# Four of six filter pieces laid out by a strided copy and a transposing DMA in place of TensorE transposes, with the first x loads moved ahead of the tables

## The chip, the cores and the metric

The kernel runs on one core of a Trainium2 chip. The metric is the device time of one execution in microseconds (us). Each number of a time below is the median of all executions, with the lowest and highest in brackets. Executions that lie over 1.5% above the fastest of the same kernel are called slow; they count in these medians, but they are left out of every ratio. The profile is one execution; its span is some 1.7 to 3.9 us shorter than the time of the same execution.

## The reference

Two independent halves share the core, and their outputs lie side by side.

```python
def _A_ref(q, k, v, shift_k, ssm_k, ssm_D):      # S = 2048, D = 576
    ... # k_shift: four taps of k along the sequence
    kv = k_shift * v
    L = 2 * S
    ... # kv and ssm_k padded to L, both through an FFT, multiplied, back
    y = y + kv * ssm_D[None, None, :]
    return q * y

def _B_ref(x, wqkv, wo):                          # 32 heads of 18
    ... # q, k, v = x @ wqkv
    phi = lambda t: jnp.where(t > 0, t + 1, jnp.exp(t)) + 1e-6
    pq, pk = phi(q), phi(k)
    kv = jnp.einsum("bhsd,bhse->bhde", pk, v)
    ... # num, den, o = num / den
    return o... @ wo
```

The first half is a long convolution. The kernel computes it with matmuls against tables of cosines and sines. For these the filter `ssm_k`, which lies in memory as channels by time, must be brought into a form with time on the partitions. The second half is linear attention: projections of x, an exponential, and small matmuls.

## The kernel before

The program first makes a list of some 550 operations. Two tables that were tuned together with it then say in which order and on which engine each is issued (`PLAN`) and where each buffer lies (`PLACES`). Each engine works through its own operations in the order of the plan.

The filter comes in six pieces of 96 channels and 2048 time steps (`hs`). A piece needs time step 16a+b to go to partition a and slot b. Before, TensorE does this with 16 transposes, each of which reads 128 elements 16 apart, in two groups of eight. ScalarE or VectorE then evicts each group from PSUM into `hT`:

```python
def h_piece(i):
    cc, hh = i // 2, i % 2
    hs = SB("hs", [96, S])
    load("hs", hs, lambda e: dma(hs.t[:], A_ssm_k[96 * i:96 * i + 96, :], e), 393216, ..., two=i < 2)
    for half in range(2):
        ps = psb(1, "hps")
        def tr(e, half=half, ps=ps):
            ...
            hv = hs.t[:].rearrange("d (a b) -> d b a", b=16)
            for j in range(8):
                nc.tensor.transpose(out=o[:, 128 * j:128 * j + 96], in_=hv[:, 8 * half + j, :], ...)
        def ev(e, half=half, ps=ps):
            ...
            copy(e, hT[cc].t[:, 8 * half:8 * half + 8, 96 * hh:96 * hh + 96], i_)
    ...  # one small add (hD) of the term D into time step 0
```

The copy helper chooses the engine's instruction:

```python
def copy(e, o, i):
    if e == "ACT":
        nc.scalar.activation(out=o, in_=i, func=ACTF.Copy)
    else:
        nc.vector.tensor_copy(out=o, in_=i)
```

In the front, the loads of x wait for a memset of one column of the same buffer (`after=[x1]`), and TensorE multiplies by a dummy operand between its first operations so that its clock stays up. `SPIN` says how many such fillers, in units of 128 columns, stand at each place:

```python
x1 = P.op(("POOL", 0.2), lambda e: nc.gpsimd.memset(x_sb.t[:, :, D:D + 1], 1.0), ..., name="x1")
SPIN = (32, 2, 2, 2, 2, 2, 2, 2, 2, 2, 2, 2, 2, 2)
```

From some 16 us on, TensorE's projections of k and q (`wk`, `wq`) interleave with the convolution. Each group of a k projection needs ScalarE to take an exponential of it out of PSUM (`ek`) and then VectorE to finish it (`pk`). Both also read PSUM, so TensorE's next group waits until VectorE is done.

## Time and profile before

| | before |
|---|---|
| time, us | 171.67 (171.38 to 171.68) |
| span of the profile, us | 171.2 |
| TensorE busy | 160.8 us, 94% |
| VectorE busy | 141.6 us, 83% |
| ScalarE busy | 112.8 us, 66% |
| bytes moved | 37.7 MB |

The view is of busy time in windows. Its columns are the window, its length, then busy time and count of instructions for TensorE, its weight loads, VectorE, ScalarE and GpSimd, then the granted clock, the DMA share and GB/s.

```profile
47.00:60.00 13.00, 12.73 (x120) 9.38 (x119) 12.58 (x15) 10.37 (x14) 5.57 (x2) 1.00 0.90 254
72.00:86.00 14.00, 14.00 (x140) 11.20 (x138) 12.68 (x11) 5.58 (x7) 0.00 (x0) 0.97 0.81 211
```

Between 47 and 60 us ScalarE has 13.00 - 10.37 = 2.6 us free. Some 2.1 us of its work there are evictions of the filter (`hT`), which the change removes. Between 72 and 86 us it has 8.4 us free.

### The profile page before, as it was taken

Reading aid. Unit: us, or ns where it says so; the run is one execution under the profiler, and the core shown is the slowest. Engines: PE = TensorE matmul, PEld = TensorE weight load, DVE = VectorE, ACT = ScalarE, POOL = GpSimd, SP = SyncE. Lnnn points to the kernel's source line nnn. Section 1 sums busy time; section 2 is a strip of 40 time slices with the busy share of each in tenths; the row PEclk is TensorE's granted clock in tenths of the full one; section 3 lists DMA queues with packets and bytes.
Section 4 is the critical chain, followed back from the end, with each engine's and each line's share of the span. In section 5 each row is a group of like instructions: output and inputs, shape, how many; then the busy total and the mean of one; then the engine's idle time right before and its main releaser. Section 6 shows DMA issues by size and latency. Waiting matters only on the chain.

```text
span 171.2 us, 3899 instructions
## 1 busy us (share of the span) xinstructions
PE 160.8 (94%) x1622; PEld 119.5 (70%) x1622; DVE 141.6 (83%) x141; ACT 112.8 (66%) x122; POOL 40.8 (24%) x28
## 2 busy tenths in 40 slices
PE   7799999999999997899999997998999999999991
PEld 2479876677667865688867885785656489978670
DVE  0224689999899999999799979899989999596690
ACT  0525965483768879735376399999999997745301
POOL 8600000800070520000069027000268000810000
PEclk9957999999999999699999999999999999999999
DMA  5999997999999623399200179999988488995375
GB/s 133 281 319 325 415 357 106 208 312 316 244 242 349 180 56 122 69 297 258 84 4 7 54 217 262 246 169 268 251 271 339 165 311 272 339 304 157 110 228 162
DMA packets 53423, 37.71 MB, mean 220 GB/s; under 512 B 32991, under 2 KB 49501, under 8 KB 52894
## 3 DMA queue, kind: packets, MB, share of 16 engines
q1 hardware_dynamic: 52574, 36.50, 76.8%
q10 hardware_dynamic: 832, 0.97, 2.3%
q8 instruction: 12, 0.20, 0.5%
q14 instruction: 5, 0.04, 0.1%
HBM read 20.16 MB, written 4.98 MB: 147 GB/s over the span
## 4 chain that ended last, share of the span: by engine, by line
PE 66%; ACT 9%; DVE 8%; DMA 6%; SPq 5%; issue 4%; ACTq 0%; DVEq 0%
PE ps_all L678 13%; PE ps_all L854 11%; PE ps_all L657 9%; PE ps_all L606 8%; PE ps_all L631 6%; PE ps_all L513 5%; PE ps_all L711 5%; DVE m L261 4%; DMA hs<-in_A_ssm_k_dram 4%; ACT Ch L254 3%; PE ps_all L564 3%; SPq L528 3%; DMA X<-sph 2%; SPq L246 2%; ACT Cu L254 2%
## 5 line engine op out<-in xcount | busy, mean ns | idle before, releaser
L261 POOL TENSOR_TENSOR v<-m,v 128x1536 bf16<-128x1536 bf16 x4 | 12.4, 3098 | 69.5 <-DVE m L261 69.5
L261 POOL TENSOR_TENSOR sph<-spu,sph 128x2048 bf16<-128x2048 bf16 x4 | 16.3, 4070 | 32.1 <-DVE pqT L841 16.8
L711 PE MATMUL ps_all<-pk,x_sb 128*128 128x288 bf16 (+1 forms) x160 | 22.0, 298 | 0.0
L854 PE MATMUL ps_all<-M,pqT 126*128 126x288 bf16 (+1 forms) x160 | 21.7, 286 | 0.0
L261 DVE TENSOR_TENSOR m<-kh,Wj 128x3072 bf16<-128x3072 bf16 x12 | 20.8, 1750 | 0.1
L513 PEld LDWEIGHTS <-Gsb 128*128 128x128 bf16 x240 | 16.7, 100 | 6.0 <-issue 3.7
L678 PE MATMUL ps_all<-xT,wq 128*126 128x512 bf16 (+1 forms) x80 | 20.5, 379 | 0.1
L657 PE MATMUL ps_all<-wk,xT 128*128 128x288 bf16 x128 | 20.1, 286 | 0.0
L711 PEld LDWEIGHTS <-x_sb 128*128 128x128 bf16 x160 | 16.2, 102 | 4.9 <-issue 0.2
L854 PEld LDWEIGHTS <-pqT 126*128 126x128 bf16 (+1 forms) x160 | 14.8, 97 | 5.7 <-issue 2.1
L678 PEld LDWEIGHTS <-wq 128*126 128x126 bf16 (+1 forms) x100 | 13.0, 131 | 7.8 <-issue 0.4
L254 ACT ACTIVATE Vt<-ps_all 128x1024 bf16<-128x1024 f32 x15 | 14.9, 1029 | 4.9 <-PE ps_all L606 3.2
L682 ACT ACTIVATE eq<-ps_all,neg 126x1024 bf16<-126x1024 f32 (+1 forms) x10 | 11.1, 1113 | 10.5 <-PE ps_all L678 10.5
L254 ACT ACTIVATE Ch<-ps_all 128x1536 bf16<-128x1536 f32 x11 | 16.2, 1511 | 2.4 <-PE ps_all L513 2.3
L606 PE MATMUL ps_all<-cst,sph 128*128 128x128 bf16 x144 | 17.1, 219 | 0.1
L606 PE MATMUL ps_all<-cst,X 128*128 128x128 bf16 x144 | 17.0, 219 | 0.0
L261 DVE TENSOR_TENSOR m<-m 128x3072 bf16<-128x3072 bf16 (+1 forms) x12 | 16.2, 1346 | 0.1
L254 ACT ACTIVATE Cu<-ps_all 128x1536 bf16<-128x1536 f32 x10 | 15.1, 1535 | 1.4 <-PE ps_all L513 1.3
L254 ACT ACTIVATE ob<-ps_all 128x576 bf16<-128x576 f32 x13 | 8.6, 663 | 9.9 <-PE ps_all L854 9.8
L657 PEld LDWEIGHTS <-xT 128*128 128x128 bf16 x128 | 12.2, 98 | 4.1 <-issue 0.8
L254 ACT ACTIVATE spu<-ps_all 128x1024 bf16<-128x1024 f32 x13 | 13.1, 1033 | 2.2 <-PE ps_all L557 2.2
L606 PEld LDWEIGHTS <-X 128*128 128x128 bf16 x144 | 14.1, 98 | 0.7 <-issue 0.3
(87 smaller groups left out, 294.5 us busy)
## 6 DMA issues: line engine op xcount, KB each, us to landing
X<-sph SPq DMA_DIRECT2D x18, 256.0 KB
hs<-in_A_ssm_k_dram SPq DMA_DIRECT2D x6, 384.0 KB
v<-in_A_v_dram SPq DMA_DIRECT2D x2, 1152.0 KB
out_dram<-ob SPq DMA_DIRECT2D x16, 144.0 KB
bct<-rden_rows SPq DMA_DIRECT2D x8, 252.0 KB
kh<-in_A_k_dram SPq DMA_DIRECT2D x1, 1584.0 KB
q<-in_A_q_dram SPq DMA_DIRECT2D x1, 1280.0 KB
out_dram<-q SPq DMA_DIRECT2D x4, 320.0 KB
```

The lines of the kernel that those rows point to most:

```text
L254: nc.scalar.activation(out=o, in_=i, func=ACTF.Copy)
L261: last[e] = (nc.gpsimd if e == "POOL" else nc.vector).tensor_tensor(**kw)
L513: nc.tensor.matmul(ps.t[:, bank, lo - 512 * bank:hi - 512 * bank], lhsT=Gsb.t[:, ri, bg, j, :], rhs=src[:, lo - CC * j:hi - CC * j], start ...
L528: load(name, None, lambda e: nc.sync.dma_start_transpose(out=dst(), in_=src()), 524288, rd=rd, wr=wr, bias=bias, issue=1.8, row=512, gap=0.3)
L564: nc.tensor.matmul(ps.t[64 * h:64 * h + 64, r, :].rearrange("p (b k) -> p b k", b=4), lhsT=W2D()[64 * r:64 * r + 64, :], rhs=cv[64 * r:64 ...
L606: nc.tensor.matmul(ps.t[:, j // 4, 128 * (j % 4):128 * (j % 4) + 128], lhsT=src.t[:, 8 * jp + j, :], rhs=W3(wi), start=(wi == 0), stop=(wi ...
L631: nc.tensor.matmul(o, lhsT=Esb.t[:, b, ri, :], rhs=vt[:, 2 * b + ri], start=(ri == 0), stop=(ri == 1))
L657: nc.tensor.matmul(ps.t[:, hh, 0:HALF], lhsT=xs(t, 128 * r, 128), rhs=wk.t[:, t, HALF * hh:HALF * hh + HALF], start=(t == 0), stop=(t == 4))
L678: nc.tensor.matmul(ps.t[0:hn, j, :], lhsT=wq.t[:, t, h0:h0 + hn], rhs=xs(t, 1024 * gp + 512 * j, 512), start=(t == 0), stop=(t == 4))
L682: P.op(("ACT", _act(1024) + 0.09), lambda e: nc.scalar.activation(out=eb.t[0:hn], in_=ps.t[0:hn], func=ACTF.Exp, bias=neg1.t[0:hn, :]), rd ...
L711: nc.tensor.matmul(ps.t[:, hh, 0:n], lhsT=x_sb.t[:, r, FT[t]:FT[t] + 128], rhs=pk.t[:, r, HALF * hh:HALF * hh + n], start=(r == 0), stop=( ...
L854: nc.tensor.matmul(ps.t[:, hh, 0:HALF], lhsT=pqT.t[0:hn, c, 128 * r:128 * r + 128], rhs=M.t[0:hn, c, HALF * hh:HALF * hh + HALF], start=(c ...
```

## The change

The intent is to take four of the six pieces off TensorE, which is the fullest engine. ScalarE permutes each piece in SBUF with one copy, and a transposing DMA (a "turn") then brings it into `hT`. Besides, the first x rows are loaded before the tables, the memset that held them comes first, only the smallest loads are issued by ScalarE, some memsets go to VectorE, one output block is cut in two, and the fillers are set anew. The whole order is tuned again.

```diff
-        return P.op({"SP": issue, "ACT": 0.52} if two else ("SP", issue), fn, ...
+        return P.op(("ACT", 0.52) if two and nb < 80000 else ("SP", issue), fn, ...
...
-        for half in range(2):
+        if i >= HP:
+            hp = SB("hp", [96, 16, 128])
+            P.op({"ACT": 0.1 + 2048 * 0.00084, "DVE": _dve(2048)}, lambda e: copy(e, hp.t[:], hs.t[:].rearrange("d (a b) -> d b a", b=16)),
+                 rd=[hs], wr=[hp], name="hperm", bias=("t%d" % cc, 0.0))
+            load("hturn", None, lambda e: nc.sync.dma_start_transpose(
+                out=hT[cc].t[:, :, 96 * hh:96 * hh + 96], in_=hp.t[:].rearrange("d b a -> d (b a)")), 393216, rd=[hp], ...
+        for half in range(2) if i < HP else ():
...
-SPIN = (32, 2, 2, 2, 2, 2, 2, 2, 2, 2, 2, 2, 2, 2)
+SPIN = (28, 1, 7, 1, 1, 1, 15, 1, 1, 1, 1, 9, 10, 1, 1, 3)
-PORT = ("tapv", "p1", "p2", "hD")
+PORT = ("tap+", "tapv", "p1", "p2", "hD")
+HP = 2
... (memsets with a choice of engine; the last output block in halves; PLAN and PLACES replaced whole)
```

## The prediction

> **What bounds the kernel now.** I read the page of the profile first (busy shares, slices), then the chain that ended last in order of time, then busy time in windows cut where that chain changes engine, then groups of instructions, and last the load queue in order of time.
>
> The slices, 4.28 us each:
>
> ```profile
> PE   7799999999999997899999997998999999999991
> DVE  0224689999899999999799979899989999596690
> ACT  0525965483768879735376399999999997745301
> PEclk9957999999999999699999999999999999999999
> DMA  5999997999999623399200179999988488995375
> ```
>
> TensorE is the first bound: nine tenths or more almost throughout. VectorE is nearly full from slice 6 to slice 33, ScalarE only from slice 23 to 33, and the load queue is full up to slice 13. The clock is low in slices 2, 3 and 16.
>
> The chain that ended last, from its start and from the middle:
>
> ```profile
> 2.19 6.00 DMA hs<-in_A_ssm_k_dram
> ...
> 11.61 1.28 PE ps_all L513 x10
> ...
> 15.55 0.67 PE ps_all L513 x10
> 16.33 1.23 PE ps_all L657 x10
> ...
> 97.99 0.48 PE ps_all L483 x8
> ...
> 100.75 0.14 ACT hT L254
> ```
>
> The reader is to see three things. The front waits for the first filter pieces (hs). The same ten matmuls of L513 take 1.28 us at 11.61 and 0.67 at 15.55: the front runs at half clock. Filter transposes (L483) and their evictions (hT) stand on the chain. The first k projection (L657) begins at 16.2 and the last matmul ends at 167.7, which leaves 3.5 us for the last eviction and store.
>
> Windows (columns: length; busy us and count for PE, PEld, DVE, ACT, POOL; granted clock; DMA share; GB/s):
>
> ```profile
> 66.15:70.00 3.85, 2.03 (x25) 1.64 (x22) 3.85 (x3) 3.85 (x4) 0.00 (x0) 0.93 0.02 6
> 99.15:117.26 18.11, 15.78 (x226) 12.94 (x225) 16.26 (x17) 17.93 (x17) 4.40 (x2) 1.00 0.96 233
> ```
>
> TensorE stands idle for 1.8 us in the first of these, waiting for ScalarE's evictions of 1.5 us each, and for 2.3 us in the second, where ScalarE is full.
>
> To turn this into a budget I summed TensorE's work from the first k projection on, each kind at its warm step in the chain: 16 k at 1.23, 10 q at 2.16, 5 G at 4.05, 16 out at 1.24, 18 i1 at 0.89, i2 9.0 in all, 22 s1 at 0.67, 36 s2 at about 0.35, 8 filter-transpose groups at 0.55, 4 x-transpose groups 1.1, kv, z, den and M 4.0. The sum is 143.1 us. Between 16.2 and 167.7 lie 151.5, so 8.4 us are bubbles and slow clock. Of these the windows show 4.8 as idle TensorE, and about 1.4 is the low clock after 70 us (32 matmuls of G took 5.50 us there and 4.11 later). So: 16.2 + 143.1 + 8.4 + 3.5 = 171.2, the span.
>
> **What the Trainium skill says.** "TensorE: Matmul & The Clock Gate", Part 1: the array runs at half clock by default and is released only after a window of some 3.4 us of sustained work. The trace agrees: the granted clock is 0.50 from 8.5 to 12.8 us, after TensorE had been idle for half of 6.4 to 8.5, and 1.00 from 15. "DMA: Bandwidth & Descriptors", section "Issuing engines are not separate DMA queues": issuing from several engines saves sequencer time only. The trace fits: the issues on ScalarE's queue took 0.2 to 0.6 us each, so moving a few of them is worth little by itself. "Advanced Engine Details and Errata", section "X-Bar Transpose (TRN2)", says transposing DMAs are as fast as plain ones. Here the trace differs: while the two transposing loads of x held the queue (26 to 30 us) only 105 GB/s moved, against 437 from 19 to 22. The measurement decides: a turn costs more of the queue than its bytes suggest.
>
> **The change, part by part.**
>
> Filter pieces. Each of six pieces is now 16 transposes and two evictions. Their groups:
>
> ```profile
> L483 PE MATMUL ps_all<-cst,hs 96*128 96x96 bf16 x96 | 8.0, 235 | 1.1 <-DMA hs<-in_A_ssm_k_dram 1.1
> L254 ACT ACTIVATE hT<-ps_all 128x768 bf16<-128x768 bf16 x6 | 4.6, 808 | 0.2 <-PE ps_all L483 0.2
> L256 DVE COPY hT<-ps_all 128x768 bf16<-128x768 bf16 x6 | 3.3, 552 | 7.3 <-PE ps_all L483 7.3
> ```
>
> Four pieces leave this path: 8 groups of 8 transposes, each 0.48 to 0.63 us on the chain, so 8 x 0.55 = 4.4 us of TensorE. All eight lie after 55 us, where nothing but TensorE's partners bounds it, so I count all 4.4. Evictions removed, by the new program order: ScalarE 4 x 0.81 = 3.2 us, VectorE 4 x 0.55 = 2.2. Added: four permuting copies of 96x2048, all on ScalarE. Its copies cost 0.81 us for 768 elements and 1.02 for 1024, so some 0.83 ns each, which makes 1.9 us a copy and 7.5 in all. They are issued among the k and q projections before 62 us, where ScalarE is busy 22.3 of 34.6 us (16.3 to 50.9): mostly hidden. Also added: four turns of 0.39 MB; turns of 0.52 MB took about 2.1 us to issue when the queue was not full. Say 2 us each, 8 us of queue. Two are needed by about 57 us, near the end of the load-bound stretch; the other two fall where the DMA share was 0.02 to 0.44.
>
> The front. The load queue before:
>
> ```profile
> 2.19 0.60 SPq L246 DMA_DIRECT2D hs<-in_A_ssm_k_dram  x1
> ...
> 4.21 0.16 POOL L308 MEMSET x_sb<- 128x16 bf16 x1
> ...
> 4.39 0.64 SPq L246 DMA_DIRECT2D x_sb<-in_B_x_dram  x1
> ```
>
> The queue stood for 1.6 us because the x loads waited for a GpSimd memset; the change makes that memset GpSimd's first operation. The new order is tables for the transpose, hs twice, all four first x loads, two pieces of G, part of k, wk. Up to wk that is 3.8 MB. At the pace of before (0.57 MB by 4.28, 1.75 by 8.5, 3.13 by 12.8, 3.88 by 15) this has landed at 14.8; the filled gap gives back some 0.5 us. TensorE can then be through with both x groups, and k begins at about 14.6 instead of 16.2: 1.6 us. The remaining work also loses the second x group, 1.1 us, which is done ahead of k in otherwise waiting time. The fillers (matmuls that keep the clock) go from 58 to 82 units of 128 columns, now put before the operations that wait for x; if they keep the clock high, the half-clock phase disappears, and the k start is limited by data alone.
>
> The middle. The first convolution input lands ahead of wk, and two taps now precede the first k evacuation on VectorE, which before sat idle a good part of the time up to 19.1 us, when its first tap ran. VectorE was then full to 86 us, and its chain led to the wait at 50 to 60 us. A start some 5 us earlier plus 2.2 us less work moves its convolutions ahead. Three small adds move to GpSimd (3.1 us each there, 0.95 on VectorE) in exchange for three products coming back: no net change. The eviction of one filter spectrum in that stretch goes to VectorE, which should take away the stall at 66 to 70 (1.9 us) and the low clock after it (1.4 us). The denominator chain comes after two G products instead of three, so the multiplication of the second output starts earlier than its 117 us.
>
> The end. The last block of the second inverse is cut in two, with smaller last stores, but the last instruction is again an output store of the attention half: the 3.5 us of tail stay.
>
> Sum: k start 14.6; work 143.1 - 4.4 - 1.1 = 137.6; bubbles 8.4 - 3.3 + 3.0 = 8.1, where 3.0 is my allowance for new waits on permuting copies, turns and a fuller ScalarE; tail 3.5. The span is 163.8, and with the 0.5 us by which the median of before exceeded its span, 164.3 us.
>
> **Rivals.** First, the turns become the bound: the copy must wait for its hs, which lands behind 11 MB of loads; ScalarE runs in order, so an early copy stalls all k and q evacuations, and the turns of the second filter block hold up the loads queued behind them. For: the queue is full to 57 us and transposes are slow. Against: the two hs loads now stand ahead of the three turns that filled the queue from 36.9 to 49. This would cost 3 to 5 us and give 167 to 169. Second, the front gains nothing: TensorE falls to half clock because x is late, as it did at 8.5 us; the front's work and fillers then stretch by about 3 us, to 167. Third, ScalarE sets the pace from 100 to 145 us whatever TensorE has to do (43.1 of 45 us busy); then the 4.4 us come back as bubbles and only the front's gain and the relief of two evictions remain: 168. Fourth, the other way: VectorE's earlier start empties nearly all bubbles, and the time is 160 to 161.
>
> **Range and chances.** The sum has most of its weight on removed work that I can count, so faster by over 2% (below 168.2) needs only 3.5 of some 7.4 us. One rival alone keeps it near the border; two together reach "same". I say 160.5 to 168.8, faster 0.79, same 0.18, slower 0.03.
>
> **What would show it.** Right: L483 with 32 matmuls instead of 96; first L657 matmul at 14 to 15 us; clock of the third and fourth slices at 8 or more; no idle gap of TensorE near the third filter spectrum; ScalarE's permuting copies at 1.9 us with little wait before them; last matmul at about 160. Wrong: copies waiting for hs, a wait of L513 for a turn, a first k after 16 us, or ScalarE full for 45 us again with more TensorE idle than 2.3 us beside it.

## More of the kernel before

A letter in the plan is the engine: P for TensorE, A for ScalarE, D for VectorE, G for GpSimd, S for the load queue.

The profile of before fell in an execution of 174.28 us, called slow.

## The result, and the profile after

| | before | after |
|---|---|---|
| time, us | 171.68 (171.38 to 172.14) | 177.38 (176.76 to 179.94) |
| span of the profile, us | 171.2 | 175.0 |
| TensorE busy, us | 160.8 | 158.6 |
| ScalarE busy, us | 112.8 | 125.6 |
| bytes moved, MB | 37.7 | 39.3 |

The changed kernel is slower: the ratio is 1.032, with an interval of 1.027 to 1.037. Ratios here are the mean time of one kernel's fast runs over the mean of the other's fast runs in the same rounds, so they are not quite the ratio of the medians. The prediction said 164.3 and a range up to 168.8. The median lies 13.1 us above the prediction and 8.6 us above its range. The profile of after is of the run of 176.76, a fast one.

The slices of the profile after, each 4.4 us long, in tenths:

```profile
PE   7999999999989397979699997889999999999991
DVE  7138995998994799895599799899998999785791
ACT  2639847556699868999886766999899869735201
PEclk9969999999999789999999999999999999999999
DMA  5999999999944598197983379999999889935355
```

Two dents are new. In slice 14 (57 to 61 us) TensorE is at 3 tenths, and the clock is at 7 and 8 tenths in slices 14 and 15. In slices 18 to 20 (74 to 87 us) TensorE, which was full there before, shows 7, 9 and 6, and VectorE falls to 5 in two of them. ScalarE is at 8 or 9 tenths beside both dents.

The groups of instructions that answer to those shown of before (columns: line, engine, operation, what is written and read, count, then busy us, mean ns, and the idle time before them):

```profile
L254 ACT ACTIVATE hp<-hs 96x2048 bf16<-96x2048 bf16 x4 | 15.8, 3956 | 0.0
...
L493 PE MATMUL ps_all<-cst,hs 96*128 96x96 bf16 x32 | 2.7, 253 | 0.0
...
L254 ACT ACTIVATE hT<-ps_all 128x768 bf16<-128x768 bf16 x2 | 1.5, 808 | 0.4 <-PE ps_all L493 0.4
```

TensorE's filter transposes went from 96 to 32, as meant. ScalarE lost four evictions of 0.81 us. It gained four copies of 3.96 us each, 15.8 us in all, where the prediction had 7.5. There is no idle time before them, so they did not wait for their data.

The windows that answer to those of before:

```profile
47.00:60.00 13.00, 9.62 (x71) 6.55 (x69) 9.45 (x10) 12.70 (x10) 3.67 (x2) 0.97 0.54 92
72.00:86.00 14.00, 10.85 (x121) 8.15 (x124) 9.74 (x10) 13.60 (x10) 0.37 (x1) 1.00 0.80 151
```

ScalarE is now the full engine in both. TensorE lost 12.73 - 9.62 = 3.1 us of work in the first and 14.00 - 10.85 = 3.2 us in the second; VectorE lost about as much in each.

How one copy does it is seen in the timeline of the first dent (start, duration, instruction, and in brackets the idle time before it with what ended it):

```profile
47.16 3.97 ACT L254 ACTIVATE hp<-hs 96x2048 bf16<-96x2048 bf16 x1
...
53.28 3.91 ACT L254 ACTIVATE hp<-hs 96x2048 bf16<-96x2048 bf16 x1
...
57.85 1.42 DVE L681 SCALAR_TENSOR_TENSOR pk<-ek,ps_all 128x576 bf16<-128x576 bf16 x2 [3.18 <-ACT ek L678]
...
59.32 1.07 PE L574 MATMUL ps_all<-ctH,cst 64*64 64x512 bf16 x8 [2.65 <-DVE pk L681]
```

The second copy holds ScalarE from 53.28 to 57.19. Four exponentials of k projections (`ek`) queue up behind it. VectorE sits idle for 3.18 us until the first of them is done, and TensorE for 2.65 us until VectorE has emptied its PSUM. The clock then follows: from 60 to 65 us it was 0.74.

The chain that ended last, in the second dent (start, duration, what):

```profile
72.40 3.98 ACT hp L254
76.38 1.40 ACT Cu L254
77.77 0.90 ACT sph L254
78.67 3.84 ACT hp L254
82.52 1.34 ACT Cu L254
```

Here the copies themselves stand on the path, end to end with evictions that TensorE waits for: 11.5 us of the chain on ScalarE alone.

To see where the lead was won and lost, I counted TensorE's remaining useful work at several moments. Every matmul that is still to come counts with its duration at full clock, and fillers count nothing. The total is 146.7 us before and 142.3 us after, so by this count the removed transposes are worth 4.4 us, as predicted. The column "before" is its second profile. (A count made again from the traces, with somewhat other durations, gives leads that differ by up to 0.3 us.)

| at, us | before | after | copies in order (e2) | copies shared (e12) |
|---|---|---|---|---|
| 25 | 131.7 | 127.5 | 127.3 | 126.2 |
| 47 | 109.5 | 105.8 | 105.5 | 104.6 |
| 60 | 97.0 | 96.7 | 93.7 | 94.7 |
| 72 | 88.7 | 88.1 | 84.0 | 85.1 |
| 86 | 74.9 | 78.1 | 70.3 | 73.1 |
| 145 | 20.0 | 24.1 | 15.8 | 18.6 |

At 47 us the changed kernel is 3.7 us ahead. Between 47 and 60 us it loses 3.4, and between 72 and 86 us it loses 3.8. It ends some 4 us behind. Those two stretches hold the four copies. The profiles are not typical runs: those of e2 and e12 are of the fastest execution of each, and that of before is of one at 172.82 us. So the lead of e2 at the end of the table, some 4 us, is more than the 2.9 us between the medians.

Last, the front. The load queue after (start, duration, issue):

```profile
2.11 1.28 SPq L246 DMA_DIRECT2D x_sb<-in_B_x_dram  x2
...
9.37 0.39 SPq L246 DMA_DIRECT2D wk<-in_B_wqkv_dram  x1
```

The first x loads are issued at 2.11 us instead of 4.39. But the load of wk, which the first k projection needs, is issued at 9.37 us instead of 5.96. The first k matmul started at 16.31 us, against 16.17 before. The prediction had 14.6.

### The profile page after: what moved, and what is told of

Read it like the earlier page. It is cut to its first block, busy times and chain, and to the rows that moved or that the text cites. A ratio compares the mean times of both kernels' runs of the same rounds, so it can differ in the third digit from the quotient of the medians.

```text
span 175.0 us, 3767 instructions
## 1 busy us (share of the span) xinstructions
PE 158.6 (91%) x1561; PEld 113.7 (65%) x1561; DVE 143.4 (82%) x142; ACT 125.6 (72%) x123; POOL 36.7 (21%) x23
## 4 chain that ended last, share of the span: by engine, by line
PE 46%; ACT 14%; DVE 3%; issue 2%; ACTq 0%; DVEq 0%
PE ps_all L870 11%; PE ps_all L616 9%; PE ps_all L727 7%; PE ps_all L646 6%; PE ps_all L523 5%; ACT hp L254 4%; PE ps_all L574 3%; ACT Cu L254 3%; ACT Ch L254 3%; PE ps_all L673 2%; ACT sph L254 2%; DVE pk L681 2%; PE ps_all L694 1%; PE ps_all L567 1%; ACT ob L254 1%
## 5 line engine op out<-in xcount | busy, mean ns | idle before, releaser
L870 PE MATMUL ps_all<-M,pqT 126*128 126x288 bf16 (+1 forms) x160 | 21.5, 286 | 0.1
L727 PE MATMUL ps_all<-pk,x_sb 128*128 128x288 bf16 (+1 forms) x160 | 20.5, 286 | 0.3 <-ACT Ch L254 0.2
L254 ACT ACTIVATE Vt<-ps_all 128x1024 bf16<-128x1024 f32 x14 | 13.8, 1025 | 6.6 <-DVE q L651 3.0
L673 PEld LDWEIGHTS <-xT 128*128 128x128 bf16 x128 | 12.8, 100 | 7.4 <-issue 3.2
L254 ACT ACTIVATE Cu<-ps_all 128x1536 bf16<-128x1536 f32 x11 | 16.1, 1500 | 0.7 <-PE ps_all L523 0.4
L264 POOL TENSOR_TENSOR X<-spu,X 128x2048 bf16<-128x2048 bf16 x3 | 12.2, 4075 | 20.7 <-DVE pqT L857 16.9
L254 ACT ACTIVATE hp<-hs 96x2048 bf16<-96x2048 bf16 x4 | 15.8, 3956 | 0.0
L254 ACT ACTIVATE Ch<-ps_all 128x1536 bf16<-128x1536 f32 x10 | 14.9, 1502 | 1.0 <-PE ps_all L523 1.0
L254 ACT ACTIVATE ob<-ps_all 128x576 bf16<-128x576 f32 x12 | 7.6, 652 | 10.3 <-PE ps_all L870 9.4
L681 DVE SCALAR_TENSOR_TENSOR pk<-ek,ps_all 128x576 bf16<-128x576 bf16 x16 | 11.9, 750 | 3.7 <-ACT ek L678 3.6
L678 ACT ACTIVATE ek<-ps_all,neg 128x576 bf16<-128x576 f32 x16 | 11.5, 737 | 4.8 <-PE ps_all L673 4.6
L254 ACT ACTIVATE sph<-ps_all 128x1024 bf16<-128x1024 f32 x14 | 14.0, 1023 | 1.1 <-PE ps_all L574 0.7
```

What stands on the lines that cost most here:

```text
L264: last[e] = (nc.gpsimd if e == "POOL" else nc.vector).tensor_tensor(**kw)
L673: nc.tensor.matmul(ps.t[:, hh, 0:HALF], lhsT=xs(t, 128 * r, 128), rhs=wk.t[:, t, HALF * hh:HALF * hh + HALF], start=(t == 0), stop=(t == 4))
L678: P.op(("ACT", _act(576) + 0.085), lambda e: nc.scalar.activation(out=eb.t[:], in_=ps.t[:, :, 0:HALF], func=ACTF.Exp, bias=neg1.t[:]), rd= ...
L681: P.op(("DVE", _dve(576)), lambda e: nc.vector.scalar_tensor_tensor(out=pk.t[:, r, 0:D].rearrange("p (h c) -> p h c", h=2), in0=eb.t[:], s ...
L727: nc.tensor.matmul(ps.t[:, hh, 0:n], lhsT=x_sb.t[:, r, FT[t]:FT[t] + 128], rhs=pk.t[:, r, HALF * hh:HALF * hh + n], start=(r == 0), stop=( ...
L870: nc.tensor.matmul(ps.t[:, hh, 0:HALF], lhsT=pqT.t[0:hn, c, 128 * r:128 * r + 128], rhs=M.t[0:hn, c, HALF * hh:HALF * hh + HALF], start=(c ...
```

## The experiments

The first theory, called A, is that the copies' own length on ScalarE costs the time. The rivals are that the turns and the fuller load queue cost it, that the front with its fillers does, and that the new order of the program does whatever the copies take (C). For e5 to e7 three of the seven executions of before were slow.

**e1_before.** No edit: the kernel before again, for a second profile.

> The kernel before, unchanged, for a profile in its fast state (the one at hand is from a run of 174.28 us, over its median of 171.67). Both theories: span about 170 us, no low clock near 70 us, first k projection at 16.2 us, last matmul near 166.5.

Measured: 172.82 us, one run, span 170.8, clock 0.97. The low clock in slice 17 (68 to 73 us; the prediction counts from 0 and calls it 16) is there again, at 6 tenths, so this expectation was wrong: it belongs to the kernel, not to a disturbed run. In its windows TensorE was busy 12.74 us of 47 to 60 and 13.82 us of 72 to 86, nearly as in the first profile, so the two dents of after are not an accident of the profile compared with.

**e2_flat.** The four copies read in order. The result is wrong, because the filter's time steps then go to wrong places. The automatic comparison with the reference passed it all the same; the likely reason is that this half of the output is small beside the tolerance. It is no valid version and serves for its time alone. It also means that the comparison cannot tell whether a version is right; for those called valid below this rests on reading the code.

```diff
-  copy(e, hp.t[:], hs.t[:].rearrange("d (a b) -> d b a", b=16))
+  copy(e, hp.t[:], hs.t[:].rearrange("d (b a) -> d b a", b=16))
```

> The changed kernel with the permuting copy reading its 2048 elements in order instead of 16 apart (result wrong on purpose; same engine, same place, same turns). Theory A (the strided reads make each copy 3.97 us, and ScalarE's in-order queue holds back the projections' evictions): copies take 1.9 us, the idle TensorE at 55-60 and 80-85 us shrinks by more than half, time 171 to 173.5. Rival B (TensorE waits for the turns or their loads, not for the copies): time within 1 us of the changed kernel, 176.4 to 178.4. Rival C (the new order itself is worse): also above 175.

Measured: 169.14 us (168.50 to 169.95), ratio 0.981 (0.975 to 0.987). The tile's own view gives the lowest, median and highest duration in ns, and the windows show what follows:

```profile
L254 ACT ACTIVATE hp<-hs x4: 1895/1897/1898, 46.9 to 71.8; 96x2048 bf16<-96x2048 bf16 x4
```

```profile
47.00:60.00 13.00, 12.19 (x90) 8.13 (x89) 13.00 (x13) 11.97 (x14) 3.98 (x3) 1.00 0.93 186
72.00:86.00 14.00, 14.00 (x176) 11.14 (x174) 13.84 (x14) 10.95 (x11) 1.03 (x2) 1.00 0.98 196
```

The same instruction on the same bytes took 1.90 us instead of 3.97 when it read in order. TensorE is back at 12.19 us in the first window and full in the second, the mean clock is 1.00, and the lead of 4 us lasts to the end (table above). Order of the program, turns, loads and fillers are those of after. So rival C and the turns cannot explain the loss: 177.38 - 169.14 = 8.2 us hang on the copies' length. The two medians are of different rounds; the ratios to before, 1.032 and 0.981, differ by 5.1% of 172, or 8.7 us, which agrees. The time is below the 171 to 173.5 that theory A expected: the length cost more than A had reckoned.

**e3_dve.** The four copies issued by VectorE at the same places of the plan.

```diff
- A320 ... A316 ... A347 ... A351
+ D320 ... D316 ... D347 ... D351
```

> The changed kernel with the four permuting copies on VectorE at the same places of the order. Theory A: a copy takes some 2.2 us there[...], ScalarE is freed of 15.8 us, VectorE gets 9 us more; time 170 to 173.5. Rival B: unchanged, 176.4 to 178.4. Rival C: above 175.

Measured: 178.43 us (178.21 to 178.56), ratio 1.035 (1.028 to 1.042).

```profile
L256 DVE COPY hp<-hs x4: 1996/2030/2753, 48.7 to 78.5; 96x2048 bf16<-96x2048 bf16 x4
```

```profile
56.10 1.12 PE L673 MATMUL ps_all<-wk,xT 128*128 128x288 bf16 x4 [2.86 <-DVE pk L681]
```

VectorE does the strided copy in 2.03 us, half of ScalarE's time, and yet the kernel is as slow as after. VectorE was full in this stretch without them (12.58 of 13 us before), and the second copy (53.39 to 55.39 us) again stands in front of the `pk` that frees TensorE's PSUM. A's expectation was missed: it is not the duration alone that counts but what else the engine has to do in that window.

**e4_pe.** The four pieces go back to TensorE, in the order of after, with one eviction for each piece.

```diff
-  hp = SB("hp", [96, 16, 128])
-  ... hperm on ScalarE, hturn on the load queue
+  hp = psb(2, "hps")
+  ... 16 transposes into hp, then one eviction of 1536 elements (two on VectorE, two on ScalarE)
```

> The changed kernel's order and front with the four pieces turned on TensorE again (16 transposes and one eviction of 1536 elements each, two on VectorE, two on ScalarE) at about the places of the copies; no copies, no turns. Theory A: TensorE gets 4.4 us more work and loses the stalls of some 8 us: 171 to 174. Rival C (the rest of the new order is worse than the old): above 175. If the rest of the new order is worth something by itself, below 170.

Measured: 181.25 us (180.87 to 181.99), ratio 1.052 (1.045 to 1.058). In TensorE's timeline:

```profile
51.46 0.65 PE L681 MATMUL ps_all<-wk,xT 128*128 128x288 bf16 x4 [1.05 <-DVE hT L256]
...
57.60 0.65 PE L681 MATMUL ps_all<-wk,xT 128*128 128x288 bf16 x4 [1.54 <-ACT hT L254]
```

TensorE waits for the evictions that I placed by hand behind VectorE's taps, in PSUM that the next projection needs. This run says that those places are bad, not that the rest of the new order is. I count it as a failed test of C. e2_flat is the test that holds.

**e5_write_strided.** The copy reads in order and writes 128 elements apart. By its access patterns it moves each element to the same place as in after.

```diff
-  copy(e, hp.t[:], hs.t[:].rearrange("d (a b) -> d b a", b=16))
+  copy(e, hp.t[:].rearrange("d b a -> d a b"), hs.t[:].rearrange("d (a b) -> d a b", b=16))
```

> The changed kernel with the permuting copy turned about: it reads hs in order and writes 128 elements apart, instead of reading 16 apart and writing in order; same result, still on ScalarE. If only strided reads are slow on ScalarE, a copy takes 1.9 us and the time is that of the copy without a stride, 168 to 170. Rival (any stride is slow there): 3.5 to 4 us a copy and 176 to 178.

Measured: 201.31 us (200.25 to 201.85), ratio 1.178 (1.168 to 1.187).

```profile
L254 ACT ACTIVATE hp<-hs x4: 9302/9327/9346, 47.1 to 95.6; 96x2048 bf16<-96x2048 bf16 x4
```

Both expectations were missed. This strided writing costs 9.33 us a copy, 4.6 ns an element, against 1.9 ns for the strided reading and 0.93 ns in order. The strides differ too (128 elements against 16), so whether the writing or the wider step costs more is not separated. The four copies grew by 4 x 5.4 = 21.5 us and the kernel by 201.31 - 177.38 = 23.9 us. With e2_flat this gives three points: 1.90, 3.97 and 9.33 us a copy make 169.1, 177.4 and 201.3 us. From the first to the second the time rises by 8.2 us for 8.3 us of copies. Nearly every microsecond of copy beyond 1.9 comes out at the end.

**e6_pool.** The copies on GpSimd, which is the emptiest engine.

```diff
+  elif e == "POOL":
+      nc.gpsimd.tensor_copy(out=o, in_=i)
- A320 ... A316 ... A347 ... A351
+ G320 ... G316 ... G347 ... G351
```

> The changed kernel with the four copies on GpSimd at the same places. Theory A (what costs is the time in which an engine that evicts the projections is held): GpSimd evicts nothing, so even a copy of 4 to 5 us is hidden, except that one small add and one hT correction queue behind it; 167.5 to 171. If the turns' lateness counts instead, L523 waits for hT and the time is above 173.

Measured: 183.31 us (182.14 to 184.21), ratio 1.071 (1.060 to 1.082). VectorE's groups in the window from 40 to 52 us, while the first two copies ran:

```profile
L266 DVE TENSOR_TENSOR v<-m,v 128x1536 bf16<-128x1536 bf16 x1 | 4.0, 4017 | 0.0
```

A's expectation of 167.5 to 171 us was missed by far. The copies took 3.90 to 5.43 us each on GpSimd, and meanwhile VectorE's product of two SBUF operands took 4.02 us instead of 0.95. One tap took 5.45 us instead of 1.75. "SBUF — State Buffer" of the Trainium skill, section "Who interferes with whom", says that a VectorE instruction with two SBUF inputs contends with a GpSimd instruction that reads SBUF. The trace agrees, with these numbers: the product began at 41.67 us, under the first copy. The rival of that expectation, that lateness of the turns counts, finds no support: in the trace's list of waits no product of the filter (L525) waits for a turn. That the held-up VectorE is what makes the whole kernel slow is read from the trace and not shown by a run of its own. The first copy started at 40.95 us, after waiting 1.47 us for `hs`: the data are there six microseconds before ScalarE's first copy of 47.16, so a late `hs` is not what delays after. After itself shows no idle time before its copies either.

**e7_split.** The first two copies in quarters of 512 elements, with ScalarE's evictions between them.

```diff
- A320 ... A316
+ A320.0 ... A320.1 ... A320.2 ... A320.3 ... (A316 likewise, evictions between)
```

> The changed kernel with the first two copies cut into quarters, each quarter followed by one of the next evictions of ScalarE; the same elements at the same stride, so the same total of some 4 us a piece plus about 0.15 us of start-up for each quarter; the two later copies are whole. If head-of-line blocking is what hurts (an eviction stuck behind 3.97 us), the gap at 55 to 60 us mostly goes: 173.5 to 175.5. If the total of ScalarE's time is what hurts, no gain: 176.5 to 178.5.

Measured: 177.31 us (176.69 to 178.25), ratio 1.037 (1.028 to 1.045).

```profile
47.00:60.00 13.00, 9.95 (x74) 6.96 (x73) 10.85 (x12) 13.00 (x16) 3.41 (x2) 0.97 0.44 71
```

Nothing is gained. ScalarE is now busy all 13.00 us, and TensorE is where it was (9.95). The first dent is therefore not only a long instruction that blocks the ones behind it. ScalarE simply has more to do there than fits: before it was busy 10.37 us, some 2.1 us of `hT` evictions go, and two whole copies add 7.9, eight quarters of some 1.15 us even 9.2.

**e8_front.** The copies as in after, and the fillers cut.

```diff
-SPIN = (28, 1, 7, 1, 1, 1, 15, 1, 1, 1, 1, 9, 10, 1, 1, 3)
+SPIN = (28, 1, 1, 1, 1, 1, 1, 1, 1, 1, 1, 1, 1, 1, 1, 1)
```

> The changed kernel with the fillers of the front cut to one unit each after the first 28 (12 units of 512 columns and 7 of 128 fewer). If the x pieces had landed and the fillers themselves held TensorE back, the first transpose of x comes before 10 us and k starts at 15 or before. If the loads set it, the first x transpose stays at about 11 us, k at about 16.3, with more idle TensorE or half clock before it.

Measured: 176.33 us, one run. TensorE's timeline:

```profile
8.98 1.06 PE L349 MATMUL ps_all<-cst,x_sb 128*128 128x128 bf16 x8
...
16.06 0.65 PE L673 MATMUL ps_all<-wk,xT 128*128 128x288 bf16 x4 [1.10 <-DMA wk<-in_B_wqkv_dram]
```

The transposes of x start at 8.98 us instead of 11.03, so x had landed and the fillers held TensorE. But the first k projection still starts at 16.06 us, because TensorE then waits 1.10 us for wk. The start of k is bound by when wk lands, not by x, fillers or clock.

**e9_flat_nofill.** Both edits at once: copies in order (wrong result) and fillers cut.

> The copy without a stride (wrong result on purpose) and the front's fillers cut as in the front test. The front test ran 1.2 us ahead in remaining TensorE work from 25 to 47 us. If the order behind it can keep that lead once the copies are short: 167.5 to 168.5, 1 us under the unstrided copy alone (169.14). If loads or VectorE set the pace from 20 us on: 169 to 170.

Measured: 168.82 us (167.41 to 172.31; the last is called slow), ratio 0.981 (0.973 to 0.988). That is the time of e2_flat. k starts at 16.14 us after 1.33 us of waiting for wk. The front gives 0.8 us more lead at 25 us and 0.3 us in the end, within the scatter. It lies between the two expectations, nearer to the one in which the front's lead does not pass through.

**e10_halves.** A valid version that shares each copy: the first half on ScalarE, the second on VectorE, and the fillers cut.

```diff
-  lambda e: copy(e, hp.t[:], hs.t[:].rearrange("d (a b) -> d b a", b=16))
+  lambda e, part=0: copy(e, hp.t[:, 8 * part:8 * part + 8], hs.t[:].rearrange("d (a b) -> d b a", b=16)[:, 8 * part:8 * part + 8])
- A320 ... A316 ... A347 ... A351
+ A320 D320.1 ... A316 D316.1 ... A347 D347.1 ... A351 D351.1
```

> Right result: each permuting copy is shared, eight of the sixteen groups on ScalarE (some 2.1 us), eight on VectorE (some 1.1 us), at the same places; fillers of the front cut. ScalarE's share is then as long as the unstrided copy that ran in 169.14, VectorE gets 4.4 us in a stretch where it is full: 170.5 to 173. If VectorE's share costs as much as the whole copy there did, 175 to 178.

Measured: 174.23 us (171.18 to 176.01), between its two expectations. Only the lowest run is fast, so there was no ratio.

**e11_before_front.** The kernel before, with the memset first on GpSimd and the fourth filler count raised from 2 to 10.

```diff
- S286 G30 S6 G3 S15 A8 G4 S280 A60 G31 A41 G0 G1 A57 G5
+ S286 G5 G30 S6 G3 S15 A8 G4 S280 A60 G31 A41 G0 G1 A57
-SPIN = (32, 2, 2, 2, 2, ...)
+SPIN = (32, 2, 2, 10, 2, ...)
```

> The kernel before with two small things of the change's front: GpSimd's memset for x first, so that the x loads are issued at about 2.8 us instead of 4.4, and 10 instead of 2 units of filler ahead of the transposes that wait for the second filter piece, to keep the clock. If loads and clock bound the front: k starts at 14.5 to 15.5 and the time is 170 to 171. If not: within 0.5 us of the kernel before.

Measured: 172.41 us (169.47 to 173.02; three of six runs slow), ratio of the fast ones 0.995 (0.986 to 1.003): the same. The edit did only half of what was meant. The memset ran at 0.74 us instead of 4.21, and the x load that ScalarE issues went out at 2.86 us instead of 4.40. But the x load on the load queue was still issued at 4.34 us, after 1.7 us of waiting for the first `hs` load to land, whose semaphore (the flag that tells of a landing) it uses again. In its profile, of a slow execution, the clock from 8.5 to 12.8 us was 0.80 instead of 0.50, and k started at 15.58 us instead of 16.17. In the time no gain could be measured; what x loads that are wholly free would give to the old kernel is not tested.

**e12_halves_again.** e10_halves unchanged, in five rounds.

> The kernel of e10_halves once more, unchanged, because only one of its four runs was fast (171.18, the others 173.92 to 176.01 at a clock of 0.971 to 0.986) and no verdict came of it. If the shared copies leave TensorE just short of its stalls, the time scatters again, median 173 to 175, ratio 1.00 to 1.015: better than the changed kernel's 1.032 and not better than before. Rival: 171.2 is what it really takes and the slow runs were chance; then most runs lie at 171 to 172 and the ratio at 0.99 to 1.00.

Measured: 173.21 us (171.09 to 174.94), beside 173.24 (171.39 to 174.92) for before on this chip; ratio 1.003 (0.998 to 1.007): the same. The first reading holds: it is better than after and not better than before. The rival was wrong: 171.1 was the lowest of eight. The profile, and so the column e12 in the table above, is of that lowest run and shows its best case.

```profile
L262 ACT ACTIVATE hp<-hs x4: 2060/2070/2101, 46.0 to 73.0; 96x1024 bf16<-96x1024 bf16 x4
L264 DVE COPY hp<-hs x4: 1066/1083/1818, 47.6 to 73.5; 96x1024 bf16<-96x1024 bf16 x4
```

```profile
47.00:60.00 13.00, 10.37 (x80) 6.98 (x79) 13.00 (x14) 10.33 (x12) 4.74 (x3) 1.00 0.98 201
```

ScalarE falls to 10.33 us in the window and VectorE is full at 13.00, yet TensorE gets only 10.37 against 12.19 in e2_flat. Two half copies on VectorE cost 2.2 us there, and TensorE loses 1.8. No valid version that I tried beats the kernel before.

## Why the prediction was wrong

**The term that failed.** It is this step of the sum: "Its copies cost 0.81 us for 768 elements and 1.02 for 1024, so some 0.83 ns each, which makes 1.9 us a copy and 7.5 in all." The per-element cost was taken from evictions out of PSUM that read in order; the new copy reads SBUF 16 elements, or 32 bytes, apart. It measured 3.96 us, or 3956 / 2048 = 1.93 ns an element, 15.8 us in all. e2_flat isolates it: with copies of 1.90 us, as predicted, the time is 169.14, just above the predicted range. Of the 13.1 us of the miss, 8.2 are this term.

The skill could have warned me. "SBUF — State Buffer", section "Door 1: The DMA port swizzle", notes that SBUF has lines of 16 bytes, that every access to a new line pays a penalty, and that bf16 can stride by up to 8 elements for free. I did not look it up. The trace agrees in kind.

**The window of the slack.** The same step went on: "They are issued among the k and q projections before 62 us, where ScalarE is busy 22.3 of 34.6 us (16.3 to 50.9): mostly hidden." The place was wrong. Only two copies ran before 62 us, at 47 to 57 us, and only 3.7 us of that lie inside the window quoted; the slack before it cannot be used, because the copies stand late in ScalarE's order. The other two ran at 72 to 83 us. But at the predicted size this would have cost little. From 47 to 60 us ScalarE had 2.6 us free and lost some 2.1 us of `hT` evictions, which holds two copies of 1.9 us and not two of 3.96. So it was measured: in e2_flat TensorE was busy 12.19 us there, against 12.73 before. What the place did was to let the excess through nearly one for one, since VectorE is as full there and both engines sit between TensorE and its next free PSUM. e3_dve, e7_split and e12_halves_again show this from three sides. For the second pair the chain shows the copies in line with evictions that TensorE waits for. No run moved or split that pair alone, so for it the blocking is read from the chain and not shown by an experiment; that their length is the cause is shown by e2_flat, where the loss from 72 to 86 us is gone.

**The front.** The step "Up to wk that is 3.8 MB ... this has landed at 14.8" failed. wk landed at 15.9 to 16.1 us in all four profiles in which TensorE waited for it (e8, e9, e10, e12). By the trace of after, 274 GB/s over the first 16.1 us, 4.4 MB had moved by then. That is 0.6 MB more than counted. A piece of G (0.26 MB) and wq were issued at 10.35 and 12.13 us, before wk was there, and shared the rate; that this is the 0.6 MB is my estimate. So k started at 16.31 instead of 14.6. The second x group was done ahead of k, as predicted: its transposes ran from 13.71 to 15.65 us, and before they came after k. But from 16 to 25 us TensorE was busy 8.50 us, against 9.00 before, with two waits of 0.25 us for evictions, and at 25 us nothing of the front's gain was left. The lead was 131.7 - 127.5 = 4.2 us, where the prediction's terms (4.4 + 1.1 + 1.6) make 7.1.

A reading of the front was wrong besides. The prediction said that the load queue stood for 1.6 us "because the x loads waited for a GpSimd memset". The trace of before has 1.3 us of this as a wait for the first `hs` load to land, and only the rest as a wait for GpSimd. e11, which took the memset away, shows the same: the queue still stood until 4.34 us.

With the copies at the predicted length, e2_flat gained 172.02 - 169.14 = 2.9 us on before, and the prediction said 7.4. The front explains some 2.7 of the missing 4.5 (the 1.1 and the 1.6): at 25 us the lead of e2_flat was 4.4, the transposes alone. The last 1.8 stay open. The prediction's offset of 0.5 us between time and span is a slip besides: it set the median of fast runs against the span of a slow one. Fast runs of before lie 2.0 to 3.7 us above their spans. This changes nothing in the result, since the predicted gain of 7.4 taken from the median of 171.67 gives 164.3 in any case.

**What was right.** The work taken off TensorE was 4.4 us, by count. The tail stayed: the last matmul began its final stretch at 167.55 and ended at 171.42, 3.6 us before the end. In after no instruction is listed as waiting for the turns:

```profile
L483 SPq DMA_TRANSPOSE hT<-hp x4: 1432/1442/1587, 51.2 to 85.2; - x4
```

They took 1.44 us each to issue, under the 2 us allowed. VectorE's first tap ran at 16.1 us instead of 19.1, earlier as foreseen, though by 3 us and not 5. The clock of the third and fourth slices was predicted at 8 or more and came as 6 and 9, against 5 and 7 before: half right, and without effect, since wk was the limit. The stall near the third filter spectrum was to disappear; from 60 to 72 us TensorE was busy 10.17 us after and 10.18 us before, and the clock was 0.89 in both, so it did not. With the short copies the clock there was 1.00, and by the table 9.7 us of work were done, against 8.3 before.

**The rivals.** The first, "the turns become the bound", had the right place (ScalarE, in order, stalling the k and q evacuations) and the wrong reason: the copies did not wait for `hs`, which e6_pool shows to have been there at 41 us, and the turns were quick. It allowed 3 to 5 us and ended at 167 to 169, so it missed as well. The second, "the front gains nothing", came true in its title, but by another cause: x was not late, and in e8_front TensorE waited for wk although the clock was low before. The third, ScalarE full from 100 to 145 us, did not happen: it was busy 39.17 us of those 45, and 43.14 before. The fourth did not happen. None of the four had asked what a strided read costs, and the chance of 0.03 for "slower" was far too small for a term that no row of the profile had ever measured.

## What to carry to other kernels

Moving work from the fullest engine to another pays only if the receiving engine has room in the very stretch where the work must run; cut that window first, and set the new instruction's length against the free time in it, less the work that goes. A copy that permutes is another instruction than a copy that does not: take its cost from a trace with the same stride, or measure it alone before tuning a whole order around it. When a load is moved forward, some other load is moved back, and the first operation after the front waits for the last of all its operands.

## What the Trainium skill lacked or had wrong

- "SBUF — State Buffer", the note on lines of 16 bytes, gives the limit of a free stride but no cost beyond it. On ScalarE, 96x2048 bf16 elements took 1.90 us read and written in order, 3.96 us read 16 elements apart, and 9.33 us written 128 elements apart: 0.93, 1.93 and 4.6 ns an element. No such size is on the page. The last two differ in direction and in step, so which of these makes the difference is open.
- No page compares the engines on such a copy; the one cost of a strided read that I found, in "GPSIMD Engine Reference", is for that engine's own kernels. Here it was 2.03 us on VectorE, 3.96 us on ScalarE, 3.90 to 5.43 us on GpSimd.
- "SBUF — State Buffer", section "Who interferes with whom", is confirmed; the size here was 4.02 us for a product of 0.95 us, and 5.45 us for a tap of 1.75 us.
- "Advanced Engine Details and Errata", section "X-Bar Transpose (TRN2)", says that transposing DMAs are as fast as plain ones. Here they were not. While the first turn from SBUF to SBUF ran (52.3 to 54.4 us of after), the DMA engines were busy 0.99 and moved 187 GB/s; plain loads in before moved 437 GB/s (19 to 22 us). While the two turns of x from memory held the queue, 105 GB/s moved, at a DMA share of 0.70. The page gives one range for both kinds.
